# Three weight chunks prepared on GpSimd, one Q load and its turn moved up, and one product put ahead of statistics, in a fused block-sparse attention and SoLU kernel

## The chip, the cores and the metric

The kernel runs on one NeuronCore of a Trainium2 chip. TensorE multiplies (PE in the profile, with its weight loads as PEld), VectorE (DVE), ScalarE (ACT) and GpSimd (POOL) compute, and SyncE (SP) issues most of the DMAs; the 16 DMA engines move the data. Every engine works through its own list of instructions in a fixed order, and instructions of different engines wait for each other through semaphores. The metric is device time in microseconds (us) of one execution, taken as the median over runs.

## The reference

Attention with a block mask, over 4 batches, 8 heads, 768 positions and 64 columns per head, followed by a dense layer with a softmax-weighted linear unit:

```
scores = scale * q @ k^T, masked by blocks of 32 (neighbours, first and last block, 3 sampled ones)
attn   = softmax(scores);   x = attn @ v            # x: 3072 tokens x 512
h      = x @ w_in                                   # 512 -> 1024
u      = h * softmax(h)
y      = ((u - mean(u)) / sqrt(var(u) + 1e-6) * g_ln) @ w_out   # 1024 -> 512
```

Inputs and output are 32-bit floats; the kernel multiplies in bf16.

## The kernel before

The work is cut in b (4 batches), pr (4 pairs of heads), t (3 tiles of 256 query rows) and, for the dense layer, 24 tiles of 128 tokens numbered j. Steps are declared as named operations with an engine and their dependencies (class `Plan`), and a written list, `ORDER`, says in which order they are recorded. That list fixes the order on every engine, SP's DMA queue included; nothing is reordered at run time. A step that needs a buffer takes the one that came free first, and waits for its last readers.

The steps that matter here, by their names in `ORDER`'s terms:

- `load4/q0.p`, `load6/k1.p` and so on (L332, on SP): loads of Q, K or V of one pair of heads into the staging buffers `qst`, `kst`, `vst`, three of each. For batch 0 the Q of a pair comes in two parts; `load4/q0.p` is the second, 256 KB.
- `cast4/q0.p.2` (L484, POOL) turns that part to bf16, `turn8/qp.2` (L439, PE) transposes it, `evac8/qp.2` (L426, DVE) copies it into `qT`, where the scores of tiles t = 1 and 2 read it.
- For batches 1 to 3, `cast6` (L495, POOL) makes bf16, `cross_kq` (L497, SP) transposes by DMA into `kx` or `qx`, and two `split` copies (L501, DVE) move it into `kT` or `qT`.
- `score/b.t.p.n` (L523, PE), `exp/b.t.p.n` (L528, ACT), `pv/b.t.p` (L542, PE), `recip` and `norm` (L551, L554, DVE): attention of one pair and tile in three thirds n. The scores use two PSUM buffers in turn, so a score waits for the exp two before it.
- `feed4/j.0`, `feed4/j.1` (L602, PE): h of tile j, in one PSUM buffer for all tiles. `silu_e/j` (L624, ACT) takes its exponential, `mult/j` (L627, DVE) makes u. Only when `mult/j` has ended can `feed4/(j+1).0` start: this is a ring of four steps through PE, ACT and DVE.
- `stats/j.0`, `stats/j.1` (L634), `aggr/j` (L637) on DVE, `z2/j`, `vr/j`, `rs/j` on POOL (L640, L643, L676): the variance of u and the factor of each row. `out4/j.0`, `out4/j.1` (L717, PE) multiply u, transposed, by the prepared second weight, four chunks of 128 rows each; `scale/j` (L723, DVE) applies the factor.
- The second weight is prepared once: eight `wsum` steps (L388, L391, DVE) add up g times w_out over its eight chunks, `whalf` (L394, L395, DVE) splits the sum in two bf16 parts, `cs` (L400, PE) sums over rows, `wbar` (L403, DVE) makes the mean, and eight `wo` steps (L405, DVE), one per chunk c, write g times w_out minus the mean as bf16. `out4/j.0` needs chunks 0 to 3, `out4/j.1` chunks 4 to 7.

Of the kernel before, what the change touches and what calls it, by code (L numbers as in the profile page):

```python
# [16 lines left out]
    1116, 0, 21, 31, 1115, 2, 115, 11, 32, 1114, 1, 3, 4, 5, 13, 33, 12, 14, 22, 15, 9, 6, 86, 16, 23, 35, 17, 116,  # L17
    18, 24, 34, 19, 10, 118, 20, 37, 25, 119, 26, 38, 121, 29, 120, 92, 1113, 117, 122, 1118, 1117, 7, 40, 123,
    127, 36, 8, 165, 41, 124, 126, 39, 167, 166, 44, 114, 135, 90, 130, 168, 45, 128, 136, 131, 169, 46, 129, 42,
    132, 170, 174, 133, 144, 137, 139, 175, 138, 176, 125, 140, 141, 87, 177, 178, 145, 43, 142, 27, 134, 146, 48,  # L20
    179, 28, 183, 147, 148, 153, 150, 184, 149, 185, 93, 30, 47, 151, 88, 84, 186, 91, 187, 89, 171, 188, 192, 172,
    173, 154, 156, 193, 194, 155, 159, 273, 49, 195, 274, 196, 94, 52, 180, 143, 197, 201, 181, 182, 157, 152, 202,
    203, 158, 275, 85, 204, 276, 205, 95, 160, 162, 206, 210, 161, 375, 189, 211, 376, 212, 190, 191, 198, 213,
    214, 55, 199, 277, 219, 215, 51, 278, 200, 207, 96, 220, 221, 208, 209, 163, 222, 279, 223, 164, 216, 224, 280,
    228, 217, 218, 229, 281, 97, 379, 98, 230, 232, 380, 231, 99, 225, 233, 237, 226, 54, 100, 388, 238, 227, 239,
    101, 234, 240, 241, 235, 102, 242, 236, 282, 103, 313, 378, 246, 283, 377, 243, 50, 104, 247, 389, 284, 288,
    384, 248, 249, 250, 397, 244, 105, 58, 297, 251, 385, 285, 255, 245, 298, 110, 256, 383, 57, 381, 257, 61, 299,
    252, 393, 107, 291, 258, 259, 286, 260, 264, 300, 265, 253, 108, 314, 292, 266, 382, 315, 267, 109, 398, 261,
    106, 316, 268, 254, 53, 386, 411, 394, 269, 321, 317, 402, 293, 412, 406, 413, 262, 287, 324, 263, 329, 289,
    387, 414, 304, 391, 415, 390, 307, 111, 407, 416, 392, 420, 308, 330, 421, 113, 403, 290, 270, 112, 331, 422,  # L30
    271, 60, 395, 424, 423, 272, 294, 400, 344, 399, 425, 396, 417, 295, 56, 429, 418, 431, 419, 296, 430, 405,
    426, 64, 409, 432, 309, 59, 427, 408, 67, 404, 433, 332, 62, 438, 434, 310, 301, 401, 439, 345, 302, 440, 303,
    428, 346, 305, 318, 441, 306, 442, 311, 410, 435, 443, 333, 312, 616, 447, 319, 339, 325, 448, 612, 436, 334,
    449, 347, 437, 65, 326, 63, 450, 451, 66, 348, 444, 452, 456, 445, 446, 360, 457, 320, 519, 349, 322, 453, 323,
    350, 620, 458, 327, 460, 459, 361, 454, 351, 328, 455, 335, 461, 355, 340, 630, 362, 465, 617, 341, 336, 337,
    466, 363, 629, 467, 613, 462, 338, 468, 364, 625, 469, 463, 520, 68, 464, 470, 352, 342, 70, 474, 365, 343,
    521, 475, 370, 476, 522, 478, 356, 626, 477, 523, 527, 353, 471, 634, 479, 483, 354, 530, 472, 366, 357, 473,
    638, 484, 480, 367, 358, 368, 485, 369, 481, 359, 482, 487, 486, 550, 535, 643, 618, 488, 492, 621, 524, 536,
    69, 493, 525, 73, 494, 622, 615, 489, 614, 495, 496, 537, 371, 627, 490, 526, 628, 501, 497, 542, 538, 635,
    528, 372, 529, 502, 503, 373, 551, 504, 491, 374, 624, 505, 72, 539, 498, 506, 75, 510, 631, 499, 500, 552,  # L40
    511, 619, 512, 545, 553, 514, 531, 513, 554, 558, 644, 639, 507, 515, 648, 508, 71, 509, 566, 649, 555, 516,
    623, 640, 650, 517, 540, 532, 651, 518, 637, 652, 581, 533, 567, 653, 541, 556, 546, 543, 534, 568, 647, 633,
    76, 657, 853, 561, 547, 569, 658, 544, 659, 636, 654, 660, 632, 548, 661, 582, 655, 662, 557, 549, 646, 559,
    641, 78, 849, 666, 656, 74, 583, 570, 667, 576, 560, 642, 668, 645, 670, 669, 562, 854, 671, 663, 79, 584, 675,
    664, 665, 563, 676, 585, 589, 573, 672, 677, 673, 592, 586, 679, 678, 597, 571, 680, 587, 684, 674, 598, 685,
    564, 686, 572, 565, 588, 681, 590, 687, 77, 574, 871, 688, 682, 599, 683, 577, 575, 756, 693, 689, 604, 591,
    578, 850, 694, 695, 579, 690, 696, 580, 697, 691, 600, 593, 698, 702, 692, 607, 594, 703, 704, 595, 706, 705,
    601, 757, 596, 80, 707, 602, 699, 82, 603, 711, 872, 700, 605, 701, 713, 606, 712, 758, 858, 714, 708, 867,
    859, 759, 715, 709, 608, 81, 716, 760, 764, 866, 720, 609, 721, 710, 767, 722, 610, 717, 723, 761, 611, 724,
    718, 762, 772, 725, 851, 729, 763, 719, 773, 765, 855, 730, 787, 876, 852, 726, 774, 868, 731, 768, 732, 775,  # L50
    779, 862, 733, 880, 738, 782, 776, 734, 769, 766, 727, 739, 740, 770, 788, 741, 777, 771, 742, 861, 789, 743,
# [72 lines left out]
def kernel(  # L124
# [17 lines left out]
    P = 128  # L142
# [672 lines left out]
```

## Time and profile before

| | |
|---|---|
| median of 3 runs | 207.35 us (206.69 to 207.46) |
| the profiled execution | 206.99 us, of which the recorded span is 205.3 |
| PE, ACT, DVE, POOL busy, share of the span | 96%, 83%, 72%, 36% |
| granted TensorE clock | full in every slice |
| bytes moved | 41.29 MB, 201 GB/s on average |

A row of the timeline gives the start in us from the span's beginning, the duration in us, the engine, the line, the operation, what it writes and reads with shapes, how many instructions were merged into it, and in brackets the idle time of the engine before it with what ended that. A row of the stretches gives, for each engine, busy microseconds and the number of instructions, then the granted clock as a share, the mean load of the DMA engines (over 1 when packets overlap) and GB/s. A row of waits gives who waited for whom, the total in us, how often, and the longest. Ends of matrix products are modelled, so their durations overlap a little; the distance from one start to the next is the better measure.

### The profile page before, as it was taken

The page shows a single profiled execution, that of the slowest core. Times are in us where ns is not written, and L with a number is a line of the kernel's source. Part 1 is how long each engine was busy: PE and PEld are TensorE (multiplying, and loading weights), DVE is VectorE, ACT ScalarE, POOL GpSimd, SP SyncE. Part 2 cuts the span into 40 slices and gives each one's busy share as a digit, 9 for nine tenths or more (in the row PEclk, how much of TensorE's full clock was granted, in tenths as well). Part 3 has the DMA queues.
Part 4 walks back from the last instruction along what each step waited for, and adds up shares of the span by engine and source line. Part 5 has one row for each costly group of instructions (what it writes and reads, how often), then busy time and mean ns, then how long its engine had stood idle before and what let it go on. Part 6 is the DMA issues. An engine that isn't in the chain of part 4 may idle for free.

```text
span 205.3 us, 5741 instructions
## 1 busy us (share of the span) xinstructions
PE 196.3 (96%) x2279; PEld 139.5 (68%) x2279; DVE 148.2 (72%) x327; ACT 170.4 (83%) x210; POOL 73.7 (36%) x153
## 2 busy tenths in 40 slices
PE   3999999989999999999999999999999999999993
PEld 1788977656867667666666766666766676676452
DVE  6486779999997676877868374689586556459863
ACT  4499989989879797998888979998988999997470
POOL 5874423446316366311430415424120301200272
PEclk9999999999999999999999999999999999999999
DMA  5999999999999999999999979956962443342233
GB/s 136 325 338 363 294 283 137 283 225 318 170 307 270 297 196 274 257 282 240 191 316 205 226 187 288 173 124 80 219 155 51 102 105 67 91 102 56 53 116 144
DMA packets 71088, 41.29 MB, mean 201 GB/s; under 512 B 52236, under 2 KB 67092, under 8 KB 71060
## 3 DMA queue, kind: packets, MB, share of 16 engines
q1 hardware_dynamic: 69968, 39.86, 81.3%
q0 software_dynamic: 1056, 1.05, 3.0%
q8 instruction: 18, 0.29, 0.7%
q14 instruction: 10, 0.08, 0.1%
q10 hardware_dynamic: 36, 0.00, 0.0%
HBM read 23.07 MB, written 6.29 MB: 143 GB/s over the span
## 4 chain that ended last, share of the span: by engine, by line
PE 63%; DMA 15%; POOL 7%; issue 6%; DVE 4%; SPq 3%; POOLq 0%; DVEq 0%; ACT 0%; ACTq 0%
PE spairs L523 20%; PE mbank L717 15%; PE hpair L602 14%; PE mbank L542 12%; DMA kst<-in_k_dram 7%; DMA qst<-in_q_dram 5%; DMA vst<-in_v_dram 3%; SPq L497 2%; POOL rs L676 2%; POOL va L418 1%; SPq L332 1%; PE sones L602 1%; POOL kb L495 1%; DVE u L654 1%; DVE ot L723 1%
## 5 line engine op out<-in xcount | busy, mean ns | idle before, releaser
L528 ACT ACTIVATE ex<-spairs 128x1024 bf16<-128x1024 f32 x144 | 141.2, 1025 | 21.6 <-PE spairs L523 19.4
L523 PE MATMUL spairs<-qT,kT 88*128 88x256 bf16 x576 | 84.1, 273 | 1.0 <-ACT ex L528 0.8
L523 PEld LDWEIGHTS <-kT 88*128 88x128 bf16 x576 | 52.7, 97 | 21.4 <-issue 2.3
L717 PE MATMUL mbank<-w_out_sb,uT 128*128 128x512 bf16 x184 | 47.1, 379 | 0.1
L602 PE MATMUL hpair<-w_in_sb,xT 128*128 128x512 bf16 x176 | 45.0, 379 | 0.7 <-DVE u L627 0.7
L542 PEld LDWEIGHTS <-ex 128*128 128x128 bf16 x1152 | 41.6, 97 | 4.6
L542 PE MATMUL mbank<-va,ex 128*128 128x65 bf16 x1152 | 43.0, 194 | 0.0
L627 DVE TENSOR_TENSOR u<-hpair,e 128x1024 bf16<-128x1024 f32 x22 | 26.8, 1217 | 12.6 <-ACT e L624 12.5
L634 DVE BATCH_NORM_STATS2 bs<-u 128x6 f32<-128x512 bf16 x44 | 29.0, 678 | 0.2
L602 PEld LDWEIGHTS <-xT 128*128 128x128 bf16 x192 | 18.4, 97 | 14.5 <-issue 0.9
L717 PEld LDWEIGHTS <-uT 128*128 128x128 bf16 x184 | 17.6, 97 | 13.6 <-issue 0.5
L723 DVE TENSOR_SCALAR ot<-mbank,rs 128x512 f32<-128x512 f32 x23 | 17.2, 748 | 11.6 <-POOL rs L676 7.3
L624 ACT ACTIVATE e<-hpair 128x1024 bf16<-128x1024 f32 x22 | 22.5, 1021 | 1.3 <-PE hpair L602 0.7
L643 POOL TENSOR_SCALAR vr<-z,mv 128x1 f32<-128x1 f32 x22 | 6.3, 287 | 44.4 <-DVE mv L637 34.8
L551 DVE RECIPROCAL r<-mbank 128x4 f32<-128x4 f32 x48 | 8.5, 176 | 17.1 <-PE mbank L542 16.9
L640 POOL TENSOR_TENSOR z<-z 128x1 f32<-128x1 f32 x22 | 4.9, 227 | 43.5 <-ACT e L624 39.0
L554 DVE TENSOR_TENSOR x<-mbank,r 128x256 bf16<-128x256 f32 x48 | 19.9, 414 | 0.8
L418 POOL CAST va<-vst 128x768 bf16<-128x768 f32 x16 | 13.7, 855 | 15.1 <-DMA vst<-in_v_dram 14.9
L676 POOL TENSOR_TENSOR rs<-vr,neg_half 128x1 f32<-128x1 f32 x24 | 14.0, 582 | 1.1
L495 POOL CAST qb<-qst 128x768 bf16<-128x768 f32 x12 | 10.3, 864 | 6.8 <-DMA qst<-in_q_dram 5.3
L495 POOL CAST kb<-kst 128x768 bf16<-128x768 f32 x12 | 10.4, 869 | 5.3 <-DMA kst<-in_k_dram 5.2
L501 DVE COPY kT<-kx 64x768 bf16<-64x768 bf16 x24 | 9.3, 386 | 1.9 <-DMA kx<-kb 1.5
(94 smaller groups left out, 119.8 us busy)
## 6 DMA issues: line engine op xcount, KB each, us to landing
vst<-in_v_dram SPq DMA_DIRECT2D x16, 384.0 KB, 5.3
out_dram<-ot SPq DMA_DIRECT2D x23, 256.0 KB, 2.6
kst<-in_k_dram SPq DMA_DIRECT2D x15, 384.0 KB, 4.4
qst<-in_q_dram SPq DMA_DIRECT2D x12, 384.0 KB, 5.0
w_out_f<-in_moe_w_out_dram SPq DMA_DIRECT2D x2, 1024.0 KB, 11.4
qst<-in_q_dram SPq DMA_DIRECT2D x4, 256.0 KB, 7.9
w_in_sb<-in_moe_w_in_dram POOLq DMA_DIRECT2D x2, 512.0 KB, 10.8
q0st<-in_q_dram SPq DMA_DIRECT2D x4, 128.0 KB, 2.8
```

What stands on the lines that cost most here:

```text
L495: ca = op(f"cast6/{nm}{b}.{pr}", "POOL", lambda o: nc.gpsimd.tensor_copy(out=cb[o.slot], in_=st[ld.slot].rearrange("p h c d -> p c h d")), ...
L523: nc.tensor.matmul(s[:, m, :], kT[0:KR, sl, jc, hh, :], qT[0:KR, sl, 2 * t : 2 * t + 2, hh, :], start=(m % 2 == 0), stop=(m % 2 == 1))
L528: exs.append(op(f"exp/{b}.{t}.{pr}.{n}", "ACT", lambda o, so=so: nc.scalar.activation(out=exb[o.slot], in_=banks("s", "pairs")[so.slot], f ...
L542: nc.tensor.matmul(acc(o)[:, qt, hh, :], exb[exs[n].slot][:, m, qt * P : (qt + 1) * P], va[i][:, 2 * pr + hh, jc, :], start=first, stop=(n ...
L554: nrm = op(f"norm/{b}.{t}.{pr}", "DVE", lambda o: nc.vector.tensor_tensor(out=xb[x_of[b, t].slot][:, :, 2 * pr * D : (2 * pr + 2) * D].rea ...
L602: nc.tensor.matmul(hb(n) if last else hb()[:, n, :], xTb[xt[0].slot][:, qt, c, :], w_in_sb[n][:, c, :], start=(c == 0), stop=(c == KD - 1))
L624: zs = op(f"silu_e/{j}", "ACT", lambda o: nc.scalar.activation(out=eb[o.slots["e"]], in_=hb().rearrange("p a f -> p (a f)"), func=ACT.Exp, ...
L627: us = op(f"mult/{j}", "DVE", lambda o: nc.vector.tensor_mul(out=ub[o.slot], in0=hb().rearrange("p a f -> p (a f)"), in1=eb[zs.slots["e"]] ...
L634: bs.append(op(f"stats/{j}.{n}", "DVE", lambda o, n=n: nc.vector.bn_stats(out=bsb[(bs[0] if bs else o).slot][:, n, :], in_=ub[us.slot][:, ...
L676: rs = op(f"rs/{j}", "POOL", lambda o: nc.gpsimd.tensor_tensor(out=rsb[o.slot], in0=vrb[vr.slot], in1=neg_half, op=ALU.pow), [vr, c2], tak ...
L717: nc.tensor.matmul(mbank[m0.slot], uTb[ut[0].slot][:, KF // 2 * n + f, :], w_out_sb[n][:, f, :], start=(n == 0 and f == 0), stop=(n == 1 a ...
L723: fo = op(f"scale/{j}", "DVE", lambda o: nc.vector.tensor_scalar(out=otb[o.slot], in0=mbank[os_[0].slot], scalar1=rsb[rs.slot], scalar2=No ...
```

## The change

Three edits, and the new `ORDER` that goes with them.

1. `wo` stays on DVE for chunks 0 to 4. For chunks 5, 6 and 7 a POOL step `wg` multiplies the chunk in place by g, and a second, `wp`, subtracts the mean and writes bf16.
2. `qst` gets a fourth buffer. `load4/q0.3` is issued before `load6/v0.3` and `load6/k1.0`, and its cast, turn and copy come earlier on POOL, PE and DVE.
3. On DVE `mult/1` comes before `stats/0.1`. Some neighbours change places with it.

```diff
     NSL = 4
+    WP = 3
...
-    qst = bufs("qst", [P, 2, NCH, D], FP32, NST)
+    qst = bufs("qst", [P, 2, NCH, D], FP32, NST + 1)
...
     wo = [op("wo", "DVE", lambda o, c=c: nc.vector.scalar_tensor_tensor(
         out=w_out_sb[c // 4][:, c % 4, :], in0=w_out_f[c // 4][:, c % 4, :], scalar=g_sb[:, c : c + 1],
-        in1=wbar, op0=ALU.mult, op1=ALU.subtract), [wb]) for c in range(KF)]
+        in1=wbar, op0=ALU.mult, op1=ALU.subtract), [wb]) for c in range(KF - WP)]
+    for c in range(KF - WP, KF):
+        wg = op("wg", "POOL", lambda o, c=c: nc.gpsimd.tensor_scalar(
+            out=w_out_f[c // 4][:, c % 4, :], in0=w_out_f[c // 4][:, c % 4, :], scalar1=g_sb[:, c : c + 1],
+            scalar2=None, op0=ALU.mult), prev)
+        wo.append(op("wp", "POOL", lambda o, c=c: nc.gpsimd.tensor_tensor(
+            out=w_out_sb[c // 4][:, c % 4, :], in0=w_out_f[c // 4][:, c % 4, :], in1=wbar, op=ALU.subtract), [wb, wg]))
```

`prev` is the last `wsum`. The list of numbers in `ORDER` says little by itself; by names, the order on the engines changes as follows, and ACT's does not.

```
SP    before: load6/v0.2, load6/v0.3, load6/k1.0, load4/q0.3, w_out (second half), load6/q1.0
      after:  load6/v0.2, load4/q0.3, load6/v0.3, load6/k1.0, w_out (second half), load6/q1.0
POOL  before: cast v0.2, cast v0.3, w_in (second half), cast4/q0.3.2, cast k1.0, q1.0, q1.1,
              z2/0, cast k1.1, q1.2, v1.0, k1.2, z2/2, cast k1.3
      after:  cast v0.2, w_in (second half), cast4/q0.3.2, cast v0.3, cast k1.0, q1.0, q1.1, wg, wg, wg,
              z2/0, cast k1.1, q1.2, wp (5), wp (6), cast v1.0, k1.2, wp (7), z2/2, cast k1.3
PE    before: score/0.1.1.1, pv/0.0.3, ..., score/0.1.2.1, turn8/q3.2, ..., feed4/0.0, score/0.1.3.1, score/0.1.3.2
      after:  score/0.1.1.1, turn8/q3.2, score/0.1.1.2, pv/0.0.3, ..., score/0.1.3.1, score/0.1.3.2, feed4/0.0
      and score/1.0.2.0, score/1.0.2.2 each one place earlier
DVE   before: wo (4), split q1.0.0, wo (1), stats/0.1, mult/1, recip, wo (2), uevac8/0, split q1.0.1, wo (3), wo (0),
              norm, split k1.1.0, mult/2, ..., split q1.1.0, wo (5), uevac8/1, wo (7), wo (6), recip/0.2.3, ...
      after:  wo (1), split q1.0.0, wo (2), mult/1, recip, stats/0.1, uevac8/0, wo (3), split q1.0.1, wo (0),
              norm, split k1.1.0, mult/2, ..., split q1.1.0, uevac8/1, wo (4), split q1.2 and k1.2, recip/0.2.3, ...
      and evac8/q3.2 and the wsum steps of chunks 2 and 3 come earlier
```

More of the change, by code (lines that the diff above doesn't have):

```diff
@@ L227 @@
     plan = Plan()
-    for nm, n in (("s", 2), ("h0", 1), ("h1", 1), ("m", 2), ("kst", NST), ("qst", NST), ("vst", NST),
+    for nm, n in (("s", 2), ("h0", 1), ("h1", 1), ("m", 2), ("kst", NST), ("qst", NST + 1), ("vst", NST),
                   ("q0st", 2), ("kb", NKB), ("qb", NKB), ("kx", NKX), ("qx", NKX), ("kc", 2), ("qc", 2), ("qr", 2),
```

104 rows, old and new, of the table ORDER are left out of this document.

## The prediction

> **What bounds the kernel now.** I read the page's busy shares first, then stretches of the span, then PE's waits, then the timelines of PE, DVE and POOL between 25 and 64 us, where the edited steps lie.
>
> ```profile
> PE 196.3 (96%) x2279; PEld 139.5 (68%) x2279; DVE 148.2 (72%) x327; ACT 170.4 (83%) x210; POOL 73.7 (36%) x153
> ```
>
> ```profile
> 30.00:37.00 7.00, 6.68 (x105) 5.27 (x104) 6.47 (x13) 6.64 (x9) 1.86 (x3) 1.00 1.17 187
> 37.00:51.00 14.00, 12.93 (x133) 8.90 (x132) 13.89 (x26) 12.48 (x16) 7.17 (x9) 1.00 1.19 272
> 51.00:63.00 12.00, 12.00 (x158) 8.72 (x156) 10.38 (x25) 9.92 (x12) 3.56 (x6) 1.00 1.05 251
> 63.00:200.00 137.00, 136.87 (x1519) 93.62 (x1517) 96.08 (x212) 118.18 (x151) 42.16 (x93) 1.00 0.77 173
> ```
>
> In the stretches the first number with a count is PE's busy time, the third DVE's. From 63 to 200 us PE is busy for 136.87 of 137.00 us at the full clock, on work that the change leaves as it is. So the end is that work's length after the moment at which PE gets to it: what counts is how many microseconds PE loses before about 63 us. From 37 to 51 us DVE is busy for 13.89 of 14.00 us, so there DVE's list sets the pace, and until 63 us the DMA engines are loaded throughout (1.05 to 1.19).
>
> ```profile
> PE spairs L523 <- ACT ex L528: 0.8, 4, 0.3
> PE hpair L602 <- DVE u L627: 0.7, 1, 0.7
> PE hfirst L439 <- POOL qr L484: 0.4, 1, 0.4
> ```
>
> ```profile
> 26.62 0.64 PE L439 MATMUL hfirst<-ident,qr 128*88 128x128 bf16 x8 [0.39 <-POOL qr L484]
> 37.67 1.03 PE L602 MATMUL hpair<-w_in_sb,xT 128*128 128x512 bf16 x4
> 43.53 1.02 PE L602 MATMUL hpair<-w_in_sb,xT 128*128 128x512 bf16 x4 [0.71 <-DVE u L627]
> 48.87 1.02 PE L602 MATMUL hpair<-w_in_sb,xT 128*128 128x512 bf16 x4
> 62.68 0.60 PE L523 MATMUL spairs<-qT,kT 88*128 88x256 bf16 x4
> 63.41 1.02 PE L717 MATMUL mbank<-w_out_sb,uT 128*128 128x512 bf16 x4
> ```
>
> PE's waits after the start-up come to 0.8 + 0.7 + 0.4 = 1.9 us, and the change aims at two of them: the turn of the fourth pair's Q (26.62) and the feed at 43.53, which waits for a product.
>
> ```profile
> 34.83 0.68 DVE L395 TENSOR_TENSOR whalf<-wsum,whalf 128x512 bf16<-128x512 f32 x1
> 35.75 0.72 DVE L501 COPY kT<-kx 64x768 bf16<-64x768 bf16 x2 [0.25 <-DMA kx<-kb]
> 36.40 1.21 DVE L627 TENSOR_TENSOR u<-hpair,e 128x1024 bf16<-128x1024 f32 x1
> 39.12 1.08 DVE L405 SCALAR_TENSOR_TENSOR w_out_sb<-w_out_f,g_sb,wbar 128x512 bf16<-128x512 f32 x1
> 40.12 0.97 DVE L501 COPY qT<-qx 64x768 bf16<-64x768 bf16 x1
> 41.02 0.73 DVE L405 SCALAR_TENSOR_TENSOR w_out_sb<-w_out_f,g_sb,wbar 128x512 bf16<-128x512 f32 x1
> 41.68 0.68 DVE L634 BATCH_NORM_STATS2 bs<-u 128x6 f32<-128x512 bf16 x1
> 42.28 1.20 DVE L627 TENSOR_TENSOR u<-hpair,e 128x1024 bf16<-128x1024 f32 x1
> 44.13 0.68 DVE L703 COPY uT<-mbank 128x1024 bf16<-128x1024 bf16 x1
> 45.23 1.86 DVE L405 SCALAR_TENSOR_TENSOR w_out_sb<-w_out_f,g_sb,wbar 128x512 bf16<-128x512 f32 x2
> 47.61 1.21 DVE L627 TENSOR_TENSOR u<-hpair,e 128x1024 bf16<-128x1024 f32 x1
> 51.64 1.50 DVE L405 SCALAR_TENSOR_TENSOR w_out_sb<-w_out_f,g_sb,wbar 128x512 bf16<-128x512 f32 x2
> ```
>
> The products `mult/0`, `mult/1`, `mult/2` end at 37.61, 43.48 and 48.82, and PE's feeds follow at 37.67, 43.53 and 48.87, 0.05 or 0.06 us later. So from 36 to 49 us the ring feed, exponential, product, feed is the path, and whatever stands ahead of a product on DVE is on it.
>
> **The Q load and its turn.** The load has a buffer of its own and no longer waits for one, so the turn's 0.39 us and part of ACT's waits go. But this gain is handed back: `mult/0` stands behind two copies that wait for the DMA into `kx` (35.75, after 0.25 us of idle DVE), and PE meets it at 37.67. What starts that DMA sooner is the cast of k1.0, no longer behind the late Q.
>
> ```profile
> 27.37 1.31 SPq L497 DMA_TRANSPOSE kx<-kb  x1
> 55.94 0.70 SPq L332 DMA_DIRECT2D vst<-in_v_dram  x1
> ```
>
> It is issued at 27.37 and the data are there at 35.75, over 8 us later, behind loads that were issued before it and still stand before it. With the DMA engines loaded at 1.17, I take an earlier issue to change its place in no queue: 0 gained, bounded by 0 and 0.39 + 0.8 = 1.2 us (the two waits above). On SP, v0.3 and k1.0 come 256 KB later, below 1 us at the 272 GB/s of the second stretch; k1.0 has its 8 us, and v0.3's product is moved behind a turn and a score. The second half of w_in passes ahead of one cast on POOL's queue. I price these at nothing; if v0.3 were late, PE would wait there under 1 us, and would give it back at 37.67 as well.
>
> **The product ahead of statistics, and fewer chunks on DVE.** `mult/1` leaves 0.60 us behind it (41.68 to 42.28).
>
> ```profile
> 40.15 1.02 ACT L624 ACTIVATE e<-hpair 128x1024 bf16<-128x1024 f32 x1
> 46.01 1.02 ACT L624 ACTIVATE e<-hpair 128x1024 bf16<-128x1024 f32 x1
> ```
>
> Its exponential ended at 41.2 (40.15 and 1.02), so 41.68 is possible. `mult/2`'s ended at 47.0, 0.6 us before its product: with one chunk of 0.73 us fewer ahead of it (four for five) DVE is there in time. By these alone `mult/2` and the feed behind it come about 0.65 us sooner. Two chunks fewer stand behind it, at 51.64 to 53.14, where PE is busy without a break; they are worth nothing at the end. The cover there is PE's own backlog; without it they'd be worth their 1.5 us.
>
> **The six POOL instructions.** Their durations first.
>
> ```profile
> 18.46 0.61 POOL L484 CAST qr<-qst 128x512 bf16<-128x512 f32 x1 [2.08 <-DMA qst<-in_q_dram]
> 33.47 0.83 POOL L495 CAST qb<-qst 128x768 bf16<-128x768 f32 x1 [0.44 <-DMA qst<-in_q_dram]
> 38.83 0.82 POOL L495 CAST kb<-kst 128x768 bf16<-128x768 f32 x1 [2.29 <-DMA kst<-in_k_dram]
> 39.60 1.28 POOL L495 CAST qb<-qst 128x768 bf16<-128x768 f32 x1
> 43.77 1.13 POOL L418 CAST va<-vst 128x768 bf16<-128x768 f32 x1 [2.88 <-DMA vst<-in_v_dram]
> 44.85 1.04 POOL L495 CAST kb<-kst 128x768 bf16<-128x768 f32 x1
> 60.74 0.82 POOL L418 CAST va<-vst 128x768 bf16<-128x768 f32 x1 [7.83 <-DMA vst<-in_v_dram]
> 83.23 0.82 POOL L495 CAST qb<-qst 128x768 bf16<-128x768 f32 x1 [1.39 <-DMA qx<-qb]
> 83.99 0.96 POOL L495 CAST kb<-kst 128x768 bf16<-128x768 f32 x1
> ```
>
> ```profile
> 83.54 1.62 DVE L501 COPY kT<-kx 64x768 bf16<-64x768 bf16 x2
> ```
>
> `wg` has one operand of 512: 0.61 us as in the cast at 18.46 (up to 0.83). `wp` reads two, for which no large POOL row stands: between 0.61 and twice that, 1.22. The casts grow by 0.22 us per 256 elements read (0.61 to 0.83), from 0.17; for 1024 read that gives 1.05, which I take. [...]
>
> POOL has room: it idles 2.29 us before 38.83 and 2.88 us before 43.77. The room is not the price. `wo` at 39.12 lasted 1.08 us instead of 0.73, beginning under the cast of 38.83; the cast at 39.60 then lasted 1.28 instead of 0.83, beginning under `wo`; the copy at 40.12 lasted 0.97 instead of 0.36. At 83.54 two copies took 1.62 us instead of 0.72 beside two casts. So a cast, and on DVE a copy from SBUF to SBUF or an instruction with two large SBUF operands, exclude each other for a whole instruction, and whoever has waited gets the next turn. Each added POOL instruction can thus hold up one DVE instruction ahead of a product.
>
> Laid against the rows:
> - Around `mult/0`: the q1.1 cast ends at 34.30, the three `wg` follow at once. The first runs to 34.9; `whalf` (wanted at 34.83, 0.68) to 35.58; the second `wg` to 36.2; the first copy (0.35) to 36.55; the third `wg` to 37.17; the second copy to 37.5. `mult/0` starts at 37.45 instead of 36.40: 1.05 us late.
> - Around `mult/1`: the four short steps between `mult/0` and `wo` (37.61 to 39.12, 1.5 us) end at 40.16. `wo` waits for the q1.2 cast (39.60, now 0.8) to 40.4 and runs to 41.1; `wp` to 42.15; the copy to 42.5; `wp` to 43.55; `wo` to 44.25. `mult/1` starts at 44.2 instead of 42.28: 1.9 us late, though statistics no longer stand ahead.
> - Around `mult/2`: `mult/1` ends at 45.4, statistics (0.60) and `uevac8/0` (0.64 to 0.68) fill DVE to 46.65; POOL has v1.0, k1.2 and the third `wp` in turn to 46.9; then `wo`, copy, `wo`, `norm` and copy (0.7 + 0.3 + 0.7 + 0.4 + 0.3) end at 49.3. `mult/2` starts at 49.25 instead of 47.61: 1.6 us late.
>
> Nothing behind `mult/2` gets this back, as PE has no gap from there on but 0.3 us at 63.41 (63.41 less 62.68, less the 0.44 that four score products take). That product waits, through POOL's `vr` and `rs` and DVE's `scale`, for the v1.2 cast at 60.74 behind its load (issued at 55.94), and SP's queue ahead of it moves with DVE's copies. Sum: +1.6 less about 0.2 there = **+1.4 us**. The profiled execution was 206.99 us, so 208.4; the median shown is 0.36 higher. I say 208.5 us. With `wp` at its ends the sum is +0.6 (0.61 us) or +1.8 (1.22 us).
>
> **Rivals.**
> - *It ends faster.* DVE holds its turn, and POOL's additions fall between. The place is `whalf` and the copies at 34.83 to 36.48, the price is the 1.05 us above, and it decides where POOL's `wg` waits instead of DVE. Then `mult/2` is 0.65 us sooner, 206.3 us; if the earlier `kx` DMA also passes on the 1.2 us of the Q edit, 205.1; the middle is 205.7. For it: DVE's list is the denser. Against it: 83.54, where turns alternated. [...]
> - *Given and taken cancel.* `wp` near 0.61 us, or `wg` colliding once instead of three times (one collision costs 0.6): between -0.4 and +0.8, 207.2 us in the middle.
> - *More goes wrong.* `wp` at 1.22 us and the SP queue late by as much, +2.2: 209.2 us.
>
> **How the numbers follow.** Forecast 0.45, cancel 0.27, faster 0.23, worse 0.05. Half a percent, 1.04 us, is about what a measurement of this kernel can tell from no change; from the median of 207.35 the bounds are 206.3 and 208.4. Slower: 0.42 + 0.02 + 0.05 = 0.49. Faster: 0.18 of the 0.23. Same: the rest, 0.33. Range 205.8 to 209.3: it reaches into the faster case and to the worse one, and leaves out about 0.2. The forecast's own range is 207.9 to 209.2.
>
> **What would show it.** In the changed kernel's timeline: the turn of Q without a wait, and the feed behind `mult/0` waiting longer than before (it has 0.06 us now); on POOL three `wg` of 0.6 us or longer and three `wp` near 1.05; `whalf`, the two `kx` copies and `wo` at 0.7 to 1.7 us instead of 0.68, 0.36 and 0.73; `mult/0`, `mult/1`, `mult/2` at 37.4, 44.2 and 49.3. A `mult/0` at or before 36.4 refutes the collision; a `kx` copy starting well before 35.75 refutes the full DMA queue. Gaps of PE after 64 us would refute the claim that only the first 63 us count.

## The result and the profile after

The changed kernel takes 209.61 us (median of 6 runs, 209.1 to 210.82), the kernel before 207.41 us beside it: a ratio of 1.011, 95% interval 1.0069 to 1.0152. That is 2.2 us slower, where 1.4 was forecast of the profiled execution, and the median lies 0.3 us above the range. The profiled execution took 210.82 us (span 209.0), the longest of the six. A few disturbed executions, among them those profiled in the first repetition of the change and in the run with three DVE writes and nothing on GpSimd, are left out of all ratios and readings, though not of the medians.

The busy shares on the page of the changed kernel:

```profile
PE 197.3 (94%) x2249; PEld 141.4 (68%) x2279; DVE 148.3 (71%) x324; ACT 171.0 (82%) x210; POOL 84.2 (40%) x159
```

POOL works 10.5 us more than before, for six instructions. The stretches, with the columns as before (after PE, PEld, DVE and ACT the fifth number with a count is POOL's):

```profile
30.00:37.00 7.00, 6.83 (x105) 5.49 (x107) 5.77 (x13) 6.60 (x7) 4.83 (x4) 1.00 1.41 232
37.00:51.00 14.00, 11.93 (x138) 8.29 (x139) 13.91 (x22) 12.41 (x17) 13.50 (x13) 1.00 0.81 202
51.00:63.00 12.00, 11.53 (x138) 8.36 (x139) 10.53 (x27) 10.08 (x12) 3.13 (x5) 1.00 1.01 224
63.00:200.00 137.00, 135.22 (x1513) 93.93 (x1535) 95.54 (x212) 117.11 (x145) 40.97 (x87) 1.00 0.79 179
```

From 37 to 51 us POOL is now as full as DVE (13.50 of 14.00, before 7.17), PE has lost 1.0 us of work there and the DMA engines have run low (0.81, before 1.19). From 63 to 200 us PE is no longer without a gap; some of the missing time is missing records (2249 of 2279), but not all, as the waits and the row at 109.31 show:

```profile
PE hpair L609 <- DVE u L634: 1.4, 3, 0.8
...
PE mbank L724 <- DVE x L561: 0.6, 1, 0.6
PE mbank L724 <- DMA uT<-u: 0.5, 1, 0.5
```

```profile
25.63 0.61 PE L446 MATMUL hfirst<-ident,qr 128*88 128x128 bf16 x8
40.50 1.02 PE L609 MATMUL hpair<-w_in_sb,xT 128*128 128x512 bf16 x4 [0.80 <-DVE u L634]
45.84 0.81 PE L609 MATMUL hpair<-w_in_sb,xT 128*128 128x512 bf16 x3 [0.19 <-DVE u L634]
50.40 1.02 PE L724 MATMUL mbank<-w_out_sb,uT 128*128 128x512 bf16 x4 [0.62 <-DVE x L561]
52.22 1.02 PE L609 MATMUL hpair<-w_in_sb,xT 128*128 128x512 bf16 x3 [0.36 <-DVE u L634]
109.31 1.04 PE L724 MATMUL mbank<-w_out_sb,uT 128*128 128x512 bf16 x4 [0.47 <-DMA uT<-u]
```

All three feeds now wait for their product, a new wait stands at the first output product (50.40), and `out4/8.0` waits at 109.31 for a transposed u, 46 us after the point from which I had taken PE's work to be unchanged. POOL and the instructions on DVE beside it:

```profile
34.51 5.47 POOL L410 TENSOR_SCALAR w_out_f<-w_out_f,g_sb 128x512 f32<-128x512 f32 x3
41.65 4.14 POOL L413 TENSOR_TENSOR w_out_sb<-w_out_f,wbar 128x512 bf16<-128x512 f32 x2
47.28 1.72 POOL L413 TENSOR_TENSOR w_out_sb<-w_out_f,wbar 128x512 bf16<-128x512 f32 x1
```

```profile
38.03 1.28 DVE L508 COPY kT<-kx 64x768 bf16<-64x768 bf16 x2
39.24 1.21 DVE L634 TENSOR_TENSOR u<-hpair,e 128x1024 bf16<-128x1024 f32 x1
42.89 1.76 DVE L406 SCALAR_TENSOR_TENSOR w_out_sb<-w_out_f,g_sb,wbar 128x512 bf16<-128x512 f32 x1
44.58 1.21 DVE L634 TENSOR_TENSOR u<-hpair,e 128x1024 bf16<-128x1024 f32 x1
47.89 1.34 DVE L508 COPY qT<-qx 64x768 bf16<-64x768 bf16 x1
50.96 1.21 DVE L634 TENSOR_TENSOR u<-hpair,e 128x1024 bf16<-128x1024 f32 x1
```

Three `wg` take 5.47 us (1.8 each, 0.61 forecast) and `wp` 1.7 to 2.5 (1.05 forecast). The two `kx` copies take 1.28 us instead of 0.72, a `wo` 1.76 instead of 0.73, a Q copy 1.34 instead of 0.35.

A difference between the two profiles is none of the change's: the first pv starts at 17.72 us, in before's at 15.17, because TensorE works at half pace up to 14.5 us (from the first of four score matmuls at 9.70 us to the next step it takes 0.86 us, in before's profile, from 9.20, 0.43). The same stretch in both, changed kernel first:

```profile
8.00:14.50 6.50, 6.50 (x50) 5.61 (x49) 2.44 (x6) 4.33 (x5) 3.90 (x8) 1.00 0.96 314
```

```profile
8.00:14.50 6.50, 6.44 (x81) 5.64 (x80) 4.78 (x11) 6.38 (x7) 5.03 (x9) 1.00 1.01 323
```

PE is busy throughout in both, with 50 matmuls in the one and 81 in the other, and the clock column says 1.00 in both. So the moments of this profile have to be read less 2.55 us, or from a run with a usual start, and its stretches above cover work that lies that much earlier in before's.

### The profile page after: what moved, and what is told of

Read it like the earlier page. It is cut to its first block, busy times and chain, and to the rows that moved or that the text cites. A ratio compares the mean times of both kernels' runs of the same rounds, so it can differ in the third digit from the quotient of the medians.

```text
span 209.0 us, 5714 instructions
## 1 busy us (share of the span) xinstructions
PE 197.3 (94%) x2249; PEld 141.4 (68%) x2279; DVE 148.3 (71%) x324; ACT 171.0 (82%) x210; POOL 84.2 (40%) x159
## 3 DMA queue, kind: packets, MB, share of 16 engines
q0 software_dynamic: 1056, 1.05, 3.0%
## 4 chain that ended last, share of the span: by engine, by line
PE 76%; DVE 11%; ACT 4%; POOL 2%; DMA 2%; issue 2%; SPq 1%; POOLq 0%; DVEq 0%; ACTq 0%
PE spairs L530 26%; PE hpair L609 15%; PE mbank L724 15%; PE mbank L549 14%; ACT ex L535 4%; PE hfirst L446 3%; DMA uT<-u 2%; DVE w_out_sb L406 2%; DVE u L634 2%; PE sones L609 1%; DVE kT L508 1%; POOL rs L683 1%; DVE u L661 1%; DVE qT L508 1%; DVE wsum L392 1%
## 5 line engine op out<-in xcount | busy, mean ns | idle before, releaser
L530 PE MATMUL spairs<-qT,kT 88*128 88x256 bf16 x576 | 86.3, 277 | 1.0 <-ACT ex L535 0.7
L724 PE MATMUL mbank<-w_out_sb,uT 128*128 128x512 bf16 x171 | 45.1, 379 | 1.7 <-DVE x L561 0.6
L609 PE MATMUL hpair<-w_in_sb,xT 128*128 128x512 bf16 x159 | 42.9, 378 | 2.2 <-DVE u L634 1.4
L502 POOL CAST qb<-qst 128x768 bf16<-128x768 f32 x12 | 10.8, 911 | 6.4 <-DMA qst<-in_q_dram 5.7
L508 DVE COPY kT<-kx 64x768 bf16<-64x768 bf16 x24 | 10.3, 430 | 1.1 <-DMA kx<-kb 0.7
```

Of the source, the lines that this page charges most:

```text
L502: ca = op(f"cast6/{nm}{b}.{pr}", "POOL", lambda o: nc.gpsimd.tensor_copy(out=cb[o.slot], in_=st[ld.slot].rearrange("p h c d -> p c h d")), ...
L530: nc.tensor.matmul(s[:, m, :], kT[0:KR, sl, jc, hh, :], qT[0:KR, sl, 2 * t : 2 * t + 2, hh, :], start=(m % 2 == 0), stop=(m % 2 == 1))
L609: nc.tensor.matmul(hb(n) if last else hb()[:, n, :], xTb[xt[0].slot][:, qt, c, :], w_in_sb[n][:, c, :], start=(c == 0), stop=(c == KD - 1))
L724: nc.tensor.matmul(mbank[m0.slot], uTb[ut[0].slot][:, KF // 2 * n + f, :], w_out_sb[n][:, f, :], start=(n == 0 and f == 0), stop=(n == 1 a ...
```

## The experiments

Three theories stood against each other. P: the six POOL steps cost the time, by holding DVE and delaying casts. S: the slow start comes with the change. Q: the moved load costs later DMA work. Two more came from the first results, L: a limit behind 63 us takes back what is won before it, and F: fewer instructions on DVE move a fetch of instructions.

### The parts of the change by themselves

**All but the POOL steps.** The changed kernel with `WP = 0`; on DVE `wo` 5, 7, 6 and 4 stand behind `mult/2`.

```diff
-    WP = 3
+    WP = 0
```

> The changed kernel with all eight wo steps on DVE again (chunks 5, 7, 6 and 4 behind mult/2), edits 2 and 3 kept. Theory P (the GpSimd steps cost the time: in the changed kernel wg lasts 1.7 us and wp 1.7 us instead of the 0.61 and 1.05 of the prediction, and each holds up a DVE step): the loss goes with them, and the early feed and the product ahead of statistics leave 206.3 to 207.2 us against 207.4 before; mult/2 ends at 48.2 to 48.8. Rival S (the start: in the changed kernel's profile TensorE works at half speed from 8.0 to 14.5 us and is 2.55 us late at 15 us): if edit 2 causes that, this kernel shows it too, the pv of the first pair starts at 17.7 instead of 15.2 us, and the time is 208.5 to 209.6. Rival Q (the moved load costs later DMA work, the wait of 0.64 us at out4/8.0 for a transposed u): about 207.9, with that wait in its profile.

208.05 us against 207.18 (ratio 1.0047, 1.002 to 1.0074). The 2.2 us are gone but for 0.9, so most of the loss belongs to the POOL steps; the gain that P expected with it (206.3 to 207.2) doesn't appear. Its first pv starts at 15.57, so S falls. The time is near the 207.9 of Q, but Q's wait at `out4/8.0` isn't in the profile.

**The POOL steps alone.** Before, with `wg` and `wp` in place of `wo` 5, 7 and 6:

```diff
-        in1=wbar, op0=ALU.mult, op1=ALU.subtract), [wb]) for c in range(KF)]
+        in1=wbar, op0=ALU.mult, op1=ALU.subtract), [wb]) for c in range(KF - WP)]
+    for c in range(KF - WP, KF):   # wg, wp as in the change
```

> The kernel before with edit 1 alone: chunks 5, 6 and 7 by wg and wp on GpSimd at the places they have in the changed kernel; loads, Q turn and the order of mult/1 and statistics as before. Theory P: 209.0 to 210.0 us, wg and wp near 1.7 us each, mult/0 as before or up to 0.5 us later, mult/2 ending at 49.8 to 51.0 instead of 48.82. Rival S: 207.2 to 207.8, as the start is as before. Rival Q: the same 207.2 to 207.8.

212.2 us (ratio 1.0233, 1.0192 to 1.0275): 5.0 us, more than twice the whole change and above the 210.0 that P allowed. PE's longest waits in it:

```profile
PE mbank L722 <- DVE x L559: 1.6, 1, 1.6
PE mbank L722 <- DMA uT<-u: 1.1, 1, 1.1
```

The wait for x is at `out4/0.0`, which takes the PSUM bank that `norm/0.2.1` frees; that norm stands on DVE behind three `wo`, of 1.49 us and of 2.43 for two, which took 0.71 and 1.86 before.

**The DVE order alone.** Before, with nothing but the order of the changed kernel around `mult/1`:

```diff
- wo(4), split q1.0.0, wo(1), stats/0.1, mult/1, recip, wo(2), uevac8/0, split q1.0.1, wo(3), wo(0), norm, split, mult/2
+ wo(1), split q1.0.0, wo(2), mult/1, recip, stats/0.1, uevac8/0, wo(3), split q1.0.1, wo(0), norm, split, mult/2
- ... wo(5), uevac8/1, wo(7), wo(6)
+ ... wo(5), uevac8/1, wo(7), wo(6), wo(4)
```

> The kernel before with nothing but the DVE order of the changed kernel around mult/1 and mult/2: wo 1, split, wo 2, mult/1, recip, stats/0.1, four wo instead of five ahead of mult/2; all eight wo on DVE. The prediction priced this at 0.65 us less. Theory P: 206.5 to 207.0 us, mult/1 ending at 42.9 and mult/2 at 48.2. Rivals S and Q say the same of it; if it stays at 207.4, the gain of that step is lost behind mult/2, and the prediction's sum was too low by this term as well.

> The DVE order alone once more, for a second profile: its first had mult/2 0.7 us sooner against the first pv and yet the same end, with a wait of 0.44 us at feed4/10.0. Rival L: such a wait behind 63 us again (0.3 us or more, for a product or a transposed u), and a time near 207.9. If the loss is chance of the start, no such wait, and the first pv late by what the time is longer.

> The DVE order alone for the third time. If its 0.4% was real: 207.4 to 208.0 us, and the profile shows where the 0.7 us gained by mult/2 are given back ahead of 55 us (the waits of 0.3 us for wo at out4/0.1 and behind it). If it was chance: 206.3 to 207.1 us, as predicted for this step.

> The DVE order alone, one more profile. If the 0.4% is made by waits ahead of 55 us, out4/2.0 stands 48.3 us or more behind the first pv (47.5 to 48.0 so far, 47.9 to 48.2 before); if by the DMA queue, a wait of 0.4 us or more at feed4/10.0 or out4/8.0; if by the start, the first pv at 16 us or later and no other difference.

207.92 us (1.0042, 1.001 to 1.0074), 207.68 in a single execution, 207.90 (1.0045, 1.0014 to 1.0076) on another chip, 207.88 in a last execution: not 0.65 us faster but 0.8 slower. Its four profiles have `mult/2` 0.7 to 1.5 us sooner against the first pv than the profile of before, and then `out4/0.1` waits 0.2 to 0.3 us for `wo`, which it doesn't before, since the fifth `wo` now stands behind `mult/2`:

```profile
PE mbank L715 <- DVE w_out_sb L403: 0.2, 1, 0.2
```

That is the last of the four; there `out4/2.0` stands 48.46 us behind the first pv, before 48.24 (47.89 in its repetition). It speaks for waits ahead of 55 us, but the first three had 47.53 to 47.97 and ran no faster at the end. Where the whole 0.8 us goes is left open. This order with all `wo` on DVE isn't the changed kernel's, which has no fifth `wo` to place.

**Edit 2 alone, and before once more.** The fourth buffer and the early load, cast, turn and copy, on DVE's order of before; and before unaltered.

```diff
-    qst = bufs("qst", [P, 2, NCH, D], FP32, NST)
+    qst = bufs("qst", [P, 2, NCH, D], FP32, NST + 1)
```

> Edit 2 alone: the fourth buffer for Q, its load, cast, turn and copy at the early places of the changed kernel; all eight wo on DVE, statistics ahead of mult/1, five wo ahead of mult/2, as before. The prediction priced this edit at nothing. Theory P says the same: 206.9 to 207.6 us, the turn without a wait, and the kx copies ahead of mult/0 waiting for the DMA up to 35.7 us again (counted with the start's shift). Rival Q1 (the 0.4 and 0.8 us of waits are won): 206.0 to 206.6. Rival Q2 (the later v0.3 and k1.0 or the denser SP queue cost): 208 to 208.7, as in the run with all edits but POOL's, and then edit 2 explains that run.

> The kernel before, unaltered, as a run of its own: 206.9 to 207.6 us. Theory P: its profile too may begin with TensorE at half speed for longer than to 8.0 us, and when the start is taken off (times counted from the first pv) out4/8.0 stands 90.2 to 90.7 us behind it, with no wait over 0.3 us behind 63 us. Rival S: the pv of the first pair starts at 15.2 us as in the first profile.

207.35 us (1.0013, 0.9985 to 1.004) and 207.01 (1.0005, 0.9976 to 1.0034) against 207.20. Edit 2 is worth nothing, as priced. What it does move is v0.3: here the POOL cast behind it and the pv behind that wait,

```profile
25.61 1.03 POOL L423 CAST va<-vst 128x768 bf16<-128x768 f32 x1 [1.74 <-DMA vst<-in_v_dram]
```

and PE stood still for 1.69 us from 25.0, more than the 1 us I had allowed. By `mult/2` this is made good: it starts 32.49 us behind the first pv, in before 32.44. The execution with this profile is still the longest of its twelve (208.68 us), by what its profile doesn't settle, and whether the others wait there too isn't known; their median is no later.

**The change once more, and without edit 2.** The last kernel is before with the POOL steps and the changed DVE order.

> The changed kernel once more, unaltered, for a second profile and more times. Theory P (the POOL steps cost the time, and the half-speed start of its first profile is chance): 208.9 to 210.0 us, wg and wp again 1.6 to 2.5 us each in place, and the pv of the first pair starting anywhere from 15.2 to 17.8 us. Rival S (the change causes the slow start): that pv starts at 17.5 us or later again.

> The changed kernel without edit 2: the six GpSimd steps and the DVE order of the changed kernel (mult/1 ahead of statistics, four wo ahead of mult/2), on the loads, casts and PE order of before. The GpSimd steps alone measured 212.2 us, the whole change 209.6. If the DVE order makes the difference (with the GpSimd steps in place a wo ahead of mult/2 costs up to 1.3 us, not 0.73, so one fewer is worth more): 209.0 to 210.3. If edit 2 makes it (mult/0 later, the first wg beside other work): 211.5 to 212.5.

> The changed kernel, one more profile. With a usual start (first pv at 15.2 to 16.2 us): mult/0, mult/1 and mult/2 starting near 38.1, 43.2 and 49.7 us as in the run with three tiny DVE writes, out4/2.0 49.0 to 49.7 us behind the first pv (47.9 to 48.2 before), an instruction packet near 104 to 106 us, and a wait of 0.6 to 1.4 us at out4/8.0; 209.0 to 210.2 us.

The change again: ratio 1.0154 (1.0104 to 1.0204; 209.35 to 211.25 us), and 210.17 in a last execution, with its first pv at 15.29. Without edit 2: 210.15 against 206.74 (1.019, 1.0147 to 1.0232). So the DVE order, which alone gains nothing, takes about 1.6 of the 5.0 us back once the POOL steps are there, because a `wo` ahead of `mult/2` then costs up to 1.5 us and one fewer stands there. Some of the 1.6 can be the clock of which the next lines speak: 4 of the 6 executions with the POOL steps alone had a mean clock of 0.992 or less, but 1 of the 6 without edit 2, and by the few others the difference to before is 4.1 and 3.1 us. In the last execution of the change `mult/0` starts at 38.15, as expected, but `mult/1` at 44.60 and `mult/2` at 50.83 are over 1 us later than expected, and `out4/8.0` had no wait. A reason is in its stretches (third column from the right: the granted clock):

```profile
36.00:37.00 1.00, 0.38 (x1) 0.10 (x1) 1.00 (x3) 0.88 (x1) 1.00 (x2) 1.00 1.09 379
...
38.00:39.00 1.00, 0.40 (x4) 0.20 (x3) 1.00 (x2) 0.94 (x2) 1.00 (x2) 1.00 1.14 383
39.00:40.00 1.00, 0.59 (x2) 0.23 (x2) 1.00 (x4) 1.00 (x2) 1.00 (x1) 0.82 1.20 289
40.00:41.00 1.00, 1.00 (x4) 0.41 (x3) 1.00 (x4) 0.00 (x0) 1.00 (x3) 0.50 1.09 377
```

PE, waiting for what DVE owes it, was busy for 0.38 to 0.85 of each microsecond from 36 to 40 us, and then the clock was granted at half up to 43 us. The feeds and scores of that time take longer (a feed 1.69 us instead of 1.02), and PE is late by itself. The profile with the POOL steps alone shows the same at another place, from 49.0 us:

```profile
48.00:49.00 1.00, 0.17 (x1) 0.10 (x1) 1.00 (x3) 0.74 (x1) 1.00 (x1) 1.00 1.74 304
49.00:50.00 1.00, 1.00 (x4) 0.36 (x3) 1.00 (x2) 0.00 (x0) 1.00 (x3) 0.50 0.67 190
```

Such waits aren't always followed by it: with the three writes (below) PE was busy for 0.38 and 0.61 from 38 to 40 us, and in the run without edit 2 for 0.07 from 47 to 48, and the clock stayed full. The mean clock was 0.992 or below in 10 of 30 executions of the kernels with `wg` and `wp` on POOL, in none of 12 with `wp` alone, in 2 of 80 of the other kernels, and in none of the kernel before's (12 here, and those beside the other runs).

### What a POOL step costs, and what it holds

> The kernel before with a tail behind its last step that leaves the output as it is: with nothing beside them, three each of wg's form (f32 in place times a scalar from memory), the same with a constant scalar, a cast f32 to bf16, wp's form (f32 minus f32 to bf16), a difference of bf16 operands, and wg's form with bf16 output, all 128x512 on GpSimd; then four wo on DVE alone; then three wg and three wp beside eight wo. If the instruction itself is long (form), wg and wp take 1.6 to 1.8 us alone as well, and a constant scalar or bf16 output shows which part of the form; if the 1.7 us of the changed kernel are waiting for DVE (lock), they take 0.6 and 1.05 us alone and 1.3 us or more beside the eight wo, and wo grows from 0.73 to 1.5 us or more.

A tail of three instructions of each kind on POOL behind the last step; the form of `wg`, of `wp`, and two to compare:

```diff
+    for i in range(3):
+        op("tail", "POOL", lambda o, i=i: nc.gpsimd.tensor_scalar(
+            out=pf[i], in0=pf[i], scalar1=g_sb[:, i : i + 1], scalar2=None, op0=ALU.mult))
...
```

```profile
204.02 4.67 POOL L778 TENSOR_SCALAR w_out_f<-w_out_f,g_sb 128x512 f32<-128x512 f32 x3
208.66 4.39 POOL L781 TENSOR_SCALAR w_out_f<-w_out_f 128x512 f32<-128x512 f32 x3
213.01 1.72 POOL L784 CAST w_out_sb<-w_out_f 128x512 bf16<-128x512 f32 x3
214.71 3.69 POOL L786 TENSOR_TENSOR w_out_sb<-w_out_f,wbar 128x512 bf16<-128x512 f32 x3
...
221.71 4.64 POOL L792 TENSOR_SCALAR w_out_sb<-w_out_f,g_sb 128x512 bf16<-128x512 f32 x3
```

With nothing beside it `wg` takes 1.56 us, 2.7 times a cast of the same size (0.57); a constant scalar (1.46) or bf16 output (1.55) makes little difference, so the multiplication by a scalar is itself the long form, for all that was varied here. `wp` takes 1.23 us, the upper end of the prediction's range.

> The kernel before with a tail that leaves the output as it is: on DVE eight bf16 copies of 768 alone, then sixteen beside four wg, sixteen beside four wp, eight wo beside four wp, eight wo beside four casts of 512. The prediction took it that a GpSimd instruction holds such a DVE instruction for its whole length: then a copy beside wg grows from 0.35 to 1.9 us, beside wp to 1.6, and a wo beside a cast from 0.68 to 1.3. Rival, from the first tail (a wo grew from 0.74 to 1.17 beside a wg of 1.56 alone): wg holds only for about 0.4 us of its length, so copies grow to 0.75 at most beside wg, and by 1.2 us beside wp.

The second tail puts DVE copies and `wo` beside four POOL instructions each:

```diff
+    for i in range(4):
+        op("tail", "POOL", lambda o, i=i: nc.gpsimd.tensor_tensor(
+            out=pb[i], in0=pf[i], in1=wbar, op=ALU.subtract))
+    for i in range(8):
+        op("tail", "DVE", lambda o, i=i: nc.vector.scalar_tensor_tensor(
+            out=db[i % 2], in0=df[0], scalar=g_sb[:, 0:1], in1=df[1], op0=ALU.mult, op1=ALU.subtract))
```

```profile
206.97 7.24 POOL L796 TENSOR_SCALAR w_out_f<-w_out_f,g_sb 128x512 f32<-128x512 f32 x4
...
216.29 5.34 POOL L803 TENSOR_TENSOR w_out_sb<-w_out_f,wbar 128x512 bf16<-128x512 f32 x4
...
226.87 5.82 POOL L810 TENSOR_TENSOR w_out_sb<-w_out_f,wbar 128x512 bf16<-128x512 f32 x4
```

```profile
207.11 8.90 DVE L799 COPY kx<-kx 128x768 bf16<-128x768 bf16 x16
...
217.50 9.09 DVE L806 COPY kx<-kx 128x768 bf16<-128x768 bf16 x16
...
228.07 8.48 DVE L813 SCALAR_TENSOR_TENSOR whalf<-wsum,g_sb,wsum 128x512 bf16<-128x512 f32 x8
```

Taken one by one, each DVE copy or `wo` that meets a `wp` waits for it whole: copies go from 0.36 to 1.30 us, `wo` from 0.74 to 1.75, and the two engines alternate, one instruction each. Beside `wg` three copies pass in each 1.84 us, at 0.72, 0.36 and 0.64: it holds DVE for some 0.6 us of its length only, in two pieces, as the rival had it. Nor are turns taken strictly beside `wg`: in the first tail eight `wo` took 6.60 us beside three `wg` of together 6.17, so more than one `wo` passed in each. Beside four casts, which took 3.20 us, eight `wo` took 6.50; in the first tail, with nothing beside them, three casts had taken 1.72 and four `wo` 2.73.

**`wg` left out.** The changed kernel without the three `wg`:

> The changed kernel without the three wg steps: chunks 5, 6 and 7 of the second weight are not multiplied by g (that part of the computation is left out); the three wp steps stay. Theory P, split in two: wg costs by holding the copies ahead of mult/0 (0.52 and 0.74 us instead of 0.35 each, about 0.6 us at mult/0) and by pushing z2/0 and the casts of k1.1 and q1.2 back by 1.3 to 2 us; without it mult/0 comes 0.5 to 0.7 us sooner against its feed and the time is 208.2 to 209.0 us. If wp alone, which holds a wo for 1.0 us and split for 1.0, makes the loss, the time stays at 209.2 to 209.8 us.

208.88 us (1.0081, 1.0042 to 1.0119). Against the first ratio of the change, 1.011, `wg` is worth 0.6 us; against the one from the same chip, 1.0154, it is 1.5. What `wp` costs is less sure: without any of the six steps, below, the ratio is 1.0072, only 0.2 us lower.

### Fewer DVE instructions, and the wait at 106 us

**Nothing on POOL, nothing in its place.** The changed kernel without the six steps, chunk 4 standing for 5 to 7:

```diff
+    wo += [wo[-1]] * WP
```

> The changed kernel without any of the six GpSimd steps, and nothing on DVE in their place: chunks 5, 6 and 7 of the second weight are not prepared and chunk 4 stands for them (that part of the computation is left out). It is the most that edit 1 could ever give. Theory P: with DVE relieved and GpSimd free, 206.3 to 207.2 us, and the changed kernel's distance to it (2.5 to 3.3 us) is the price of the six steps. Rival L (a limit behind 63 us, the DMA queue around 100 us, takes back what is won before): 207.2 to 208.0, with PE waiting 0.4 us or more at feed4/10.0 or out4/8.0.

207.94 us against 206.74 (1.0072, 1.0042 to 1.0101), as L had it. Relieved of three `wo`, with POOL free, the kernel is slower than before, with PE waiting 0.64 us for the transposed u at `out4/8.0`. Every profile so far with five `wo` on DVE and full clock had that wait, none with eight.

**Three `wo` out of before, and three tiny DVE writes into the others.**

```diff
+        in1=wbar, op0=ALU.mult, op1=ALU.subtract), [wb]) for c in range(KF - 3)]
+    wo += [wo[-1]] * 3
```

> The kernel before without the wo steps of chunks 5, 6 and 7 (chunk 4 stands for them, that part of the computation is left out) and nothing else changed. By the prediction's pricing that is worth nothing: 207.0 us. Theory F: it is slower than before by 0.5 to 1.0 us, 207.6 to 208.1, with the instruction packet near 105 us and PE waiting 0.6 us or more at out4/8.0. Rival R says the same of the wait; without it (0.0 to 0.2 us) both fall.

```diff
+    tiny = const.tile([P, 3], FP32, name="tiny")
+    for i in range(3):
+        op("pad", "DVE", lambda o, i=i: nc.vector.memset(tiny[:, i : i + 1], 1.0))
```

> The run without the six GpSimd steps and without wo of chunks 5 to 7 (chunk 4 stands for them, that part of the computation is left out), plus three DVE writes of one column each behind uevac8/1, so that DVE has as many instructions as before. Theory F (three DVE instructions fewer move a fetch of instructions from 100 to 105.5 us, where it delays the load q3.1 and the transposed u behind it): the instruction packet is back at 99 to 102 us, load q3.1 takes 3.6 to 3.9 us from issue to landing instead of 4.7, out4/8.0 does not wait, 207.0 to 207.5 us. Rival R (a relieved DVE shifts the DMA traffic itself): packet back, but out4/8.0 still waits 0.5 us or more and the time stays at 207.9.

> The changed kernel plus three DVE writes of one column each behind uevac8/1. Theory F: no wait at out4/8.0, and 0.5 to 1.0 us less than the changed kernel on the same side of its comparison: ratio to before 1.006 to 1.010, 208.4 to 209.2 us. Rival R: 209.6 to 210.2 us, ratio 1.011 to 1.016, with the wait.

Before with three `wo` less: 208.02 us against 207.15 (1.0078, 1.0044 to 1.0112), slower by 0.9 for less work. The kernel without POOL steps, with three writes of 0.06 us added: 206.81 (1.0007, 0.9976 to 1.0039), the 0.7% gone. The changed kernel with the three writes: 209.05 (1.0128, 1.0082 to 1.0173). In the first of the three, the window of 8 us from 98.5 of the DMA view, in 40 slices, its loads with us to landing, and PE's row:

```profile
GB/s 23 31 14 18 183 272 285 273 265 233 359 360 389 307 149 38 61 69 177 353 361 392 316 291 285 125 6 15 8 8 8 10 18 204 291 410 379 440 364 376
...
qst<-in_q_dram SPq DMA_DIRECT2D x1, 384.0 KB, 5.4
```

```profile
106.30 1.04 PE L716 MATMUL mbank<-w_out_sb,uT 128*128 128x512 bf16 x4 [1.28 <-DMA uT<-u]
```

From 103.7 to 105.1 us (a slice is 0.2 us) the DMA engines move 6 to 18 GB/s. The load of q3.1, issued just ahead of the transposed u, lands after 5.4 us instead of 3.6, and PE waits 1.28 us. In the same view of the kernel before:

```profile
GB/s 78 15 23 23 31 13 19 271 300 271 152 9 8 8 133 291 380 369 451 351 384 392 399 399 366 278 284 288 292 387 399 420 330 154 169 200 169 361 392 330
...
qst<-in_q_dram SPq DMA_DIRECT2D x1, 384.0 KB, 3.6
```

Here that gap stands at 100.7 to 101.3, and nothing is waited for. (The gap at the left of both views, up to 99.3 and 99.9, is common to them.) The queue that carries instructions has its packet just ahead of the gap that moves. One microsecond of the kernel of before, from 99.6, and one of the kernel with three `wo` less, from 103.2:

```profile
q1 hardware_dynamic: 780, 0.19, 129.4%
q14 instruction: 1, 0.01, 2.0%
```

```profile
q1 hardware_dynamic: 375, 0.11, 258.7%
q14 instruction: 1, 0.01, 1.9%
```

The same packet is at 105.5 without the POOL steps and at 106.7 in the changed kernel, and in the changed kernel with the three writes it is back at 101.2, the load takes 3.8 us and PE goes through `out4/8.0` without a wait. Over all usable profiles it lies at 99.3 to 101.7 us where DVE has all its instructions (11 profiles), none of which waits at `out4/8.0`, and at 103.7 to 106.9 where DVE has three fewer (7); six of these wait there, for 0.47 to 1.28 us. The seventh is the last execution of the change, without a near standstill behind the packet. So the first half of theory F holds: the number of instructions on DVE sets when this block of instructions is fetched.

The second half, that the fetch holds the data back, rests on where the packet lies, up to 1.2 us ahead of a near standstill of 0.5 to 1.4 us. Why one packet of 0.01 MB should do this isn't settled; there are gaps without such a packet too. By time F is borne out without the POOL steps, where the writes take the 0.7% off (that run has no usable profile). In the changed kernel the wait goes, but the ratio of 1.0128 lies above the 1.006 to 1.010 that F gave.

In the profile of before with three `wo` less, `out4/2.0` stands 46.96 us behind the first pv (48.24 and 47.89 in the two profiles of before) and `out4/8.0`, behind its wait, 90.61 (90.44 and 90.10): PE was about 1 us ahead and lost it there. That the missing `wo` won this microsecond isn't shown, since `mult/1`, ahead of which none is missing, is that early too (26.09, before 27.11 and 27.02); this kernel with the three writes was not run.

## Why the prediction was wrong

The forecast was a loss of 1.4 us, made by POOL steps that hold up DVE ahead of the products. The kind and the place of the loss came out, the size did not: 2.2 us. The step that failed is that only PE's losses ahead of 63 us count, each at its own length; and the prices of `wg` and `wp` were too low, which another error hid. How much of the missing 0.8 us each makes can't be told from the scatter of the executions. (The 208.5 that was named is also 0.25 below the sum from the median, 207.35 and 1.4.)

- **The size of the POOL steps.** With the fetch back in its place, the changed kernel costs 1.9 us (209.05 against 207.15; by the ratio 2.7), and the same kernel without the six steps nothing (206.81): they cost 2.2 us by the medians, where the prediction's own collisions came to 1.6 at `mult/2`. Two of the six executions behind the 209.05 had a mean clock of 0.992 (209.70 and 210.23 us); the median of the other four is 208.9. The profiled one of these ends 191.4 us behind its first pv, before 190.1 and 189.8: 1.3 to 1.6 us, which is what the sum gave. With the fetch moved on both sides the steps cost less, 0.8 to 1.7 us (from 1.0072 without them to 1.011 and 1.0154): the two losses don't add, probably because a PE that comes late has less to wait for at `out4/8.0`. In the profile with the three writes, its start 0.55 us late,

```profile
37.10 1.10 DVE L506 COPY kT<-kx 64x768 bf16<-64x768 bf16 x2
38.13 1.21 DVE L632 TENSOR_TENSOR u<-hpair,e 128x1024 bf16<-128x1024 f32 x1
...
43.17 1.21 DVE L632 TENSOR_TENSOR u<-hpair,e 128x1024 bf16<-128x1024 f32 x1
...
49.69 1.21 DVE L632 TENSOR_TENSOR u<-hpair,e 128x1024 bf16<-128x1024 f32 x1
```

the three products start, less 0.55, at 37.6, 42.6 and 49.1 us; forecast were 37.45, 44.2 and 49.25. But this is luck, two errors that cancel. `wg` was put at 0.61 us, from a cast of the same size, and takes 1.56 alone and up to 2.1 here; it was also taken to hold DVE for its whole length, and holds it for about 0.6. `wp` at 1.05 takes 1.23 alone, up to 2.46 with its waits. Three `wg`, 5.5 us on end, push z2/0, the casts of k1.1 and q1.2 and with them the first `wp` back (it starts at 42.33), so that no `wp` but only the casts stand in the way of `mult/1`, which so came sooner than forecast.
- **"The end is that work's length after the moment at which PE gets to it."** This step failed. Behind 63 us the work is the same but not the fetch of instructions: three `wo` fewer move it from 100 to 104 to 107 us, into the transfer that `out4/8.0` waits for. It goes with 0.9 us where it is alone (three `wo` less in before) and with 0.7% in the kernel without POOL steps. In the changed kernel it shows as the 0.47 us of wait at 109.31; by the times of the whole change it can't be told from their scatter.
- **PE's waits were counted once.** This is the same step's other half. In a third of the executions with the POOL steps the mean clock fell to 0.992 or less, and where two of these were profiled, waits of PE were followed by 3.4 us of half clock ((1 - 0.82) / 0.5 + 3.0, up to 43 us, in the one). No step of the prediction had this. What makes the clock fall isn't shown: in the one profile PE was still busy for 0.38 to 0.85 of each microsecond ahead of it.
- **The product ahead of statistics and one `wo` fewer, -0.65.** Not confirmed by itself (+0.8, with the fifth `wo` placed behind; the cause is open). Beside the POOL steps the order saves 1.0 to 1.6; there the error was to price a `wo` at 0.73, when it costs up to 1.76.
- **Edit 2 at nothing.** Right by time. The turn goes without a wait (25.63), and what PE loses to the later v0.3 in the run with edit 2 alone is made good by `mult/2`. Whether an earlier DMA helps the `kx` copies wasn't seen: DVE came to them late in every run with edit 2.
- **The rivals.** "Ends faster" needed DVE to hold its turn at `whalf` and the copies; beside `wg` it can pass, as the tails show, but here the two copies still took 1.10 to 1.28 us. "Cancel" needed `wp` near 0.61 or one collision; neither is so. "More goes wrong" gave +2.2 us, which is what was measured, and had `wp` at 1.22 us, where it is alone; but that is luck too, for it made the rest of a wait at `out4/2.0`, and the two usable profiles of the change have none there. Only the run without `wg` has one, of 0.47 us.

At most the change could have brought nothing that shows: with the three chunks removed from both engines, edits 2 and 3 kept and the fetch in its place, the kernel is as fast as before (206.81 against 207.15, ratio 1.0007, 0.9976 to 1.0039). No version here beats the kernel before.

## What to carry to other kernels

Before moving work to GpSimd, remove it and measure: here the DVE time that was to be freed was worth nothing that could be measured, so every price for it was a loss. Take the duration of a GpSimd instruction from a row of the same operation, not of the same size (here `wg` took 1.56 us, a cast of its size 0.57), and count beside it what DVE has in flight: here a copy of 0.36 us took 1.30 beside a `wp`, which held it to its end, and 0.97 beside a cast; a `wg` held DVE for some 0.6 us. And a change in the number of instructions can move the instruction fetches, here from 100 us to 104 to 107; when a wait appears far from the edit, look where they lie before looking for a cause in the data, and pad to test it.

## What was not expected of the hardware

- A fetch of 0.01 MB of instructions goes with a near standstill of the DMA queues: 6 to 18 GB/s for 1.4 us in one run, 8 to 9 GB/s for 0.6 us in another. A load across it took 5.4 us instead of 3.6.
- Waits of PE were followed by 3.4 us at half clock in two profiles, behind 4 us at 0.38 to 0.85 busy and behind 2 us at 0.20 and 0.17; in others like them they were not. The mean clock says that a third of the executions with the POOL steps had such a stretch.
- The start: the first group of four score matmuls that takes 0.6 us instead of 1.0 came anywhere from 8.0 to 14.5 us, in kernels of every kind, with PE busy from 5 us on. The granted clock in the stretches is 1.00 all the time and doesn't show it. It is one part of the scatter of 2 to 3 us between executions, and costs less than it delays: in the second tail's run, on the kernel before, the first pv was 2.4 us late (17.57) and the last output product 0.4 us.
